# Linear attention, a channel MLP and a switched expert MLP on one core: GpSimd's drains tied to its loads, a clock for transfers, more slack for ScalarE in the order of side work

## The chip, the cores and the metric

The kernel runs on one core of one Trainium2 chip. The metric is the device time in microseconds (us), taken as the median of several runs. The core's engines each have an instruction queue of their own and work in order: TensorE (PE, matmuls), VectorE (DVE), ScalarE (ACT), GpSimd (POOL) and SyncE (SP, which here only issues transfers). They wait for each other through semaphores.

## The reference

Three stages follow each other. B=4 sequences, S=576 tokens, 8 heads of 64, model width 512.

```python
def phi(x):
    proj = einsum('bhsd,df->bhsf', x, w_phi)
    proj = proj - max(abs(proj), axis=-1)
    return concat([exp(proj), exp(-proj)])
num = q_p @ (k_p^T v);  den = q_p . sum(k_p) + 1e-6      # x = num / den
u = x + (x^T @ U @ V)^T
x = u + relu(u @ w_ch1) @ w_ch2                           # 512 -> 2048 -> 512
...
e = argmax(logits) or the token before's expert           # by a local gate
out = p[e] * (relu(x @ w1[e]) @ w2[e])                    # 512 -> 1024 -> 512, 8 experts
```

## The kernel before

**Stages.** Attention runs first, with the first pass of the channel MLP (FFN) already mixed into it. From about 207 us on, TensorE runs matmuls of passes one after another, 20 passes in all, numbered 0 to 19 here. Passes 0 to 11 are the FFN: 4 units of hidden channels (512 each) times 3 pieces of tokens (768 each). Passes 12 to 19 are the experts: for each of the 4 sequences, 2 units of 512 hidden channels of one expert. A pass is some 180 or 192 matmuls: the first product, ReLU, then the second product, `mm2`, whose results DVE adds into `y`. Passes 0 to 3 and all expert passes are plain (`plain_steps`, 192 matmuls); passes 4 to 11 use a seven-product scheme (`seven_steps`, 180 matmuls), in which DVE adds partial sums `u` in PSUM between the products.

**Number format.** Every operand of these matmuls is split into two float32r tiles, a high and a low part, so each product is three matmuls. The splits are the side work: ACT casts the high part (`CAST w<-row`, L338; `CAST x<-y`, L506), POOL or DVE subtracts it from the value to get the low part (`w<-row,w`, `x<-y,x`; POOL in halves, each a 128x256 instruction for weights). FFN weights arrive as 64-bit numbers and are first narrowed to float32 by six DVE operations (`narrow`, L88 to L101) and a POOL addition in two halves (`row<-row,row`). Split activations `x` are written to DRAM (`xd`) by SP and loaded again by POOL (`x_load`, L568, 768 KB each).

**The order.** Nothing is scheduled at run time. While the program is built, `work` emits TensorE's matmuls in order, and `side` after each step lets generators (`threads`) emit side work. They decide by a clock that the build keeps: `free[engine]` says when an engine would be done, `touched[tile]` when a tile would be ready. `gate` lets an instruction out if its engine would finish it by TensorE's clock plus `SLACK[engine][step]`, a table with one row per engine and a column per step (column 8 for all steps of a plain pass); `either` picks POOL or DVE by the earlier end, with a bias of 1.0 us against DVE. A transfer's landing is a guess at issue: TensorE's clock, or the tile's last use, plus 4.5, 5.0, 6.0 or 6.5 us.

**Drains.** `paused` issues POOL's elementwise instruction and, where `pauses[0]` is set (passes 0 to 2 and from pass 10 on), a POOL `drain` after it (L72).

**Buffers.** 8 `row` tiles for narrowing and sums, 14 weight tiles `w`, 9 activation tiles `x`, 8 PSUM banks `psf` used in rotation, and seven half buffers (`raw` and `row`) into which SP loads expert weights.

Of the kernel before, what the change touches and what calls it, by code (L numbers as in the profile page):

```python
# [39 lines left out]
def model(ctx, tc, kq, vx, wphi, ident, up, vp, wff, wg, wmoe1, wmoe2, rconst, outT):  # L40
    nc = tc.nc
# [12 lines left out]
    def f32(ap):  # L54
        return ap.bitcast(F32)
# [8 lines left out]
    rawfree = [raw_p.tile([128, 1024], U32, name=f"raw{n}") for n in range(2)]  # L64

    pauses = [False]

    def paused(eng, **kw):

        eng.tensor_tensor(**kw)  # L70
        if eng is nc.gpsimd and pauses[0]:
            nc.gpsimd.drain()  # L72

    def in_halves(eng, dst, a, b, n, op):
# [67 lines left out]
    def x_tile(pool, n):  # L142
# [7 lines left out]
    late = {}  # L150
# [8 lines left out]
    emitted = [0]  # L159
    SYNC = 0.15  # L160
    SLACK = {"DVE": (2.0, 0.4, 1.5, 0.3, 0.0, 0.0, 0.0, 1.0, 2.5, 2.5, 2.5, 2.5, 2.5, 2.5, 2.0),
             "ACT": (0.3, 1.0, 1.0, 1.0, 0.5, 0.0, 0.5, 1.0, 1.0, 1.0, 1.0, 1.0, 1.0, 1.0, 1.0),
             "POOL": (2.0,) * 15}
    BIAS = 1.0
    at_step = [7]
# [15 lines left out]
    def gate(eng, dur, *keys):  # L181

        if not late:
            yield "step"
        while late and not force[0]:
            at = max([free[eng]] + [touched.get(id(k), 0.0) for k in keys])
            if at + (0.0 if eng == "POOL" else dur) <= free["PE"] + SLACK[eng][at_step[0]]:
                break
            yield "wait"
        emitted[0] += 1  # L190
        force[0] = False
        if late:
            book(eng, dur, *keys)

    def either(eng, n, *keys):

        if not late:
            yield "step"
            emitted[0] += 1
            return eng  # L200
        while True:
            best = None
            for e, name, bias in ((nc.gpsimd, "POOL", 0.0), (nc.vector, "DVE", BIAS)):
                dur = cost(name, n)
                at = max([free[name], port[0]] + [touched.get(id(k), 0.0) for k in keys])
                ok = at + (0.0 if name == "POOL" else dur) <= free["PE"] + SLACK[name][at_step[0]]
                if (ok or force[0]) and (best is None or at + dur + bias < best[0]):
                    best = (at + dur + bias, e, name, dur)
            if best is not None:
                break  # L210
            yield "wait"
        emitted[0] += 1
        force[0] = False
        free[best[2]] = max(free[best[2]], port[0])
        port[0] = book(best[2], best[3], *keys)
        return best[1]

    def spawn(kind, due, gen):
        threads.append((due, len(threads) + 1000 * emitted[0], kind, gen))
# [43 lines left out]
    def later(on, issue):  # L263

        if late:
            waiting.append((touched.get(id(on), 0.0), issue))
        else:
            issue()
# [21 lines left out]
    def raw_dma():  # L290

        while order and rawfree and (not late or force[0] or touched.get(id(rawfree[0]), 0.0) <= free["PE"] + 0.5):
            u, name = order.pop(0)
            i = (BLOCKS + VS).index(name)
            t = rawfree.pop(0)
            if wff.dtype == F32:
                nc.sync.dma_start(out=t.bitcast(F32)[:, :512], in_=wff[u.g, i])
            else:
                nc.sync.dma_start(out=t, in_=wff[u.g, i].bitcast(U32))
            touched[id(t)] = max(free["PE"], touched.get(id(t), 0.0)) + 4.5  # L300
            raws.append((u, name, t))

    pieces = {}
# [138 lines left out]
    def w_moe(u, due):  # L442

        if not loading:
            assert not order and len(rawfree) == 2
            halfraw.extend(t.bitcast(F32)[:, 512 * m:512 * m + 512] for t in rawfree for m in range(2))
        if u.b not in ereg:
            ereg[u.b] = nc.sync.value_load(pidx[u.b][0:1, 0:1], min_val=0, max_val=NE - 1)
        e = bass.ds(ereg[u.b], 1)
        todo_ = list(PLAIN)  # L450
        ahead_ = []
        loading.append(todo_)
        while len(halfraw) < 7 and len(loading) == 1 and len(rows) > 5:
            halfraw.append(rows.pop()[:, :512])
        before = loading[:-1]

        def load():
            halfraw.sort(key=lambda t: touched.get(id(t), 0.0))
            while halfraw and todo_ and not any(before) and (force[0] or touched.get(id(halfraw[0]), 0.0) <= free["PE"] + 0.5):
                name = todo_.pop(0)  # L460
                t = halfraw.pop(0)
                if name[0] == "A":
                    j0, kh = 4 * u.g + 2 * (int(name[1]) - 1), int(name[2]) - 1
                    nc.sync.dma_start(out=t.rearrange("p (j c) -> p j c", j=2),
                                      in_=wmoe1[e, j0:j0 + 2, kh].rearrange("o j p c -> p (o j) c"))
                else:
                    nc.sync.dma_start(out=t, in_=wmoe2[e, 4 * u.g + int(name[1])].rearrange("o p f -> (o p) f"))
                touched[id(t)] = max(free["PE"], touched.get(id(t), 0.0)) + 5.0
                ahead_.append(t)

        def get(name):
            load()
            while not ahead_:
                yield "blocked"
                load()
            return ahead_.pop(0)

        for s in PLAIN:
            f = yield from get(s)
            spawn("w", due, w_end(u, s, f, nc.gpsimd, halfraw))  # L480
# [19 lines left out]
    def x_end(key, s, r, keep, own=None, then=None):  # L500

        x = xo.setdefault(key, {})[s] = yield from take(xfree)
        n_ = CH if key[0] == "m" else TW
        keys = (x,) if own is None else (x, own)
        yield from gate("ACT", cost("ACT", 2 * n_), *keys)
        nc.scalar.copy(out=x[:, 0, :, :n_], in_=r)  # L506
        for k in range(2):
            use = yield from either(nc.gpsimd, n_, *keys)
            paused(use, out=x[:, 1, k, :n_], in0=r[:, k], in1=f32(x[:, 0, k, :n_]), op=ALU.subtract)
        if keep:  # L510
            later(x, lambda: nc.sync.dma_start(out=f32(xd[key[1]][XD.index(s)]), in_=f32(x)))
        xdone.add((key, s))
        if then is not None:
            then()
# [10 lines left out]
    def x_sums(key, due):  # L525

        got = {}

        def load(s):
            r = got[s] = yield from take(rows)  # L530
            while touched.get(id(r), 0.0) > free["PE"] + 0.5 and not force[0]:
                yield "wait"
            k, t = spot(key, s)
            nc.sync.dma_start(out=as_x(r), in_=ud[:, k, t])
            emitted[0] += 1
            touched[id(r)] = max(free["PE"], touched.get(id(r), 0.0)) + 6.0

        def sub(out, a, c):
            for k in range(2):
                use = yield from either(nc.gpsimd, TW, out, a, c)  # L540
                paused(use, out=as_x(out)[:, k], in0=as_x(a)[:, k], in1=as_x(c)[:, k], op=ALU.subtract)

        def end(s, r, then=None):
            spawn("x", due, x_end(key, s, as_x(r), True, r, (lambda: rows.append(r)) if then is None else then))

        for s in ("B12", "B11", "B22"):
            yield from load(s)
        yield from sub(got["B11"], got["B12"], got["B11"])
        yield from sub(got["B12"], got["B22"], got["B12"])
        yield from sub(got["B22"], got["B22"], got["B11"])  # L550
        end("T2", got["B22"], lambda: None)
        end("T1", got["B11"])
        end("T3", got["B12"])
        yield from load("B21")
        yield from sub(got["B21"], got["B22"], got["B21"])
        while (key, "T2") not in xdone:
            yield "wait"
        rows.append(got["B22"])
        end("T4", got["B21"])

    def x_load(key, names=XS):

        for s in names:
            x = xo.setdefault(key, {})[s] = yield from take(xfree)
            while touched.get(id(x), 0.0) > free["PE"] + 0.3 and not force[0]:
                yield "wait"
            yield from gate("POOL", 1.0, x)
            nc.gpsimd.dma_start(out=x, in_=xd[key[1]][XD.index(s)])  # L568
            touched[id(x)] = max(free["PE"], touched.get(id(x), 0.0)) + 6.5
            xdone.add((key, s))  # L570

    def need_x(key, s):
# [763 lines left out]
    nc.vector.memset(late["lg"], 0.0)  # L1336
    nc.gpsimd.memset(late["tr"], 0.0)
    free.update(PE=0.0, DVE=0.0, ACT=1.0, POOL=2.0)
    touched.clear()
    for k in range(8):  # L1340
        ps_at[k] = 0.0
    for k in hat:
        hat[k] = 0.0
    nc.sync.dma_start(out=ud[:, :, 3 * S:], in_=y[:, :, 3 * S:])
    spawn("x", 2, x_plain(("p", 2), BS))
    spawn("w", 3, fetch(units[1], PLAIN))
    spawn("w", 3, w_ffn(units[1], 3))
    for _ in todo:
# [141 lines left out]
```

## Time and profile before

| | us |
|---|---|
| median of 3 runs (range) | 790.01 (789.01 to 790.75) |
| profiled execution, its own time | 789.29 |
| its span, first to last instruction | 787.5 |
| TensorE busy in it | 766.6 (97%) |
| DVE, ACT, POOL busy | 493.4, 300.4, 323.8 |
| mean granted TensorE clock | 0.995 |

TensorE is the engine to watch: with 97% busy, only what lies in its idle time, or in time at a lower clock, can be won without taking work away from it. A busy share of another engine says little by itself; what counts is the stretch in which TensorE waits for it.

### The profile page before, as it was taken

What the parts mean: (1) busy time and instruction counts of PE and PEld (TensorE: products, weight loads), DVE (VectorE), ACT (ScalarE), POOL (GpSimd) and SP (SyncE); (2) the same over time, 40 slices, a digit from 0 to 9 for tenths busy, and PEclk for the clock granted to TensorE, in tenths of its full rate; (3) what the DMA queues carried; (4) which work ended last, traced back from release to release, by engine and by line L of the source; (5) the groups of instructions that cost most, each with busy time, mean ns of one, the idle gap of its engine ahead of it and who ended that gap; (6) DMA issues with size and microseconds to landing.
All of it is one profiled execution on the core that took longest, in us unless ns stands there. A gap on an engine that the chain in (4) does not pass through costs nothing.

```text
span 787.5 us, 19160 instructions
## 1 busy us (share of the span) xinstructions
PE 766.6 (97%) x7776; PEld 742.8 (94%) x7776; DVE 493.4 (63%) x951; ACT 300.4 (38%) x682; POOL 323.8 (41%) x411
## 2 busy tenths in 40 slices
PE   8999999999999999799999999999999999999997
PEld 6899888999999998799999999999999999999997
DVE  7899999743388389768797865256653831615312
ACT  5667776652232131213123122023444353353330
POOL 0212423112257476764268442002436555555242
PEclk9999999999999999899999999999999999999999
DMA  6444556222243545683436527452443233523301
GB/s 198 151 124 164 204 177 224 67 101 82 101 159 99 211 174 196 253 283 138 171 110 219 224 81 234 164 164 81 130 172 108 87 109 96 179 82 90 123 19 63
DMA packets 45114, 114.33 MB, mean 145 GB/s; under 512 B 5024, under 2 KB 21536, under 8 KB 45024
## 3 DMA queue, kind: packets, MB, share of 16 engines
q1 hardware_dynamic: 36416, 82.74, 31.1%
q0 software_dynamic: 5152, 26.89, 10.2%
q10 hardware_dynamic: 3456, 3.46, 1.3%
q8 instruction: 62, 1.02, 0.5%
q14 instruction: 28, 0.23, 0.1%
HBM read 81.47 MB, written 31.60 MB: 144 GB/s over the span
## 4 chain that ended last, share of the span: by engine, by line
PE 69%; DVE 12%; issue 8%; POOLq 6%; ACT 2%; POOL 2%; DMA 1%; SPq 0%; DVEq 0%; ACTq 0%
PE psf L1077 9%; PE psf L1078 9%; PE psf L1079 9%; PE psf L961 9%; PE psf L962 8%; PE psf L963 8%; POOLq L72 6%; PE kv L699 4%; PE num L733 3%; PE pj L666 3%; PE tq L713 2%; DVE row L96 1%; DVE y L933 1%; DVE row L91 1%; PE tps L759 1%
## 5 line engine op out<-in xcount | busy, mean ns | idle before, releaser
L1077 PE MATMUL psf<-hhi,w 128*128 128x384 f32 (+1 forms) x640 | 204.8, 320 | 1.1 <-ACT w L338 0.6
L1078 PE MATMUL psf<-hhi,w 128*128 128x384 f32 (+1 forms) x640 | 203.8, 318 | 0.5 <-POOL w L70 0.5
L1079 PE MATMUL psf<-hlo,w 128*128 128x384 f32 (+1 forms) x640 | 203.7, 318 | 0.0
L961 PE MATMUL psf<-x,w 128*128 128x384 f32 (+1 forms) x608 | 195.5, 322 | 7.4 <-DVE u L933 5.0
L962 PE MATMUL psf<-x,w 128*128 128x384 f32 (+1 forms) x608 | 194.0, 319 | 0.0
L963 PE MATMUL psf<-x,w 128*128 128x384 f32 (+1 forms) x608 | 194.0, 319 | 0.0
L935 DVE SCALAR_TENSOR_TENSOR hlo<-psf,hhi 128x384 fp32r<-128x384 f32 (+1 forms) x160 | 78.8, 512 | 134.5 <-ACT hhi L949 134.5
L70 POOL TENSOR_TENSOR row<-row,row 128x256 f32<-128x256 f32 (+1 forms) x108 | 92.5, 876 | 115.0 <-DVE row L101 99.3
L949 ACT ACTIVATE hhi<-psf 128x384 fp32r<-128x384 f32 (+1 forms) x160 | 69.9, 462 | 181.8 <-PE psf L963 101.2
L961 PEld LDWEIGHTS psf<-x,w 128*128 128x128 f32 x608 | 114.7, 189 | 10.5 <-DVE u L933 5.7
L1077 PEld LDWEIGHTS psf<-hhi,w 128*128 128x128 f32 x640 | 120.1, 188 | 3.2 <-DVE hlo L935 1.3
L1078 PEld LDWEIGHTS psf<-hhi,w 128*128 128x128 f32 x640 | 120.1, 188 | 0.7 <-POOL w L70 0.7
L1079 PEld LDWEIGHTS psf<-hlo,w 128*128 128x128 f32 x640 | 120.1, 188 | 0.0
L962 PEld LDWEIGHTS psf<-x,w 128*128 128x128 f32 x608 | 114.8, 189 | 0.3 <-POOL x L70 0.3
L963 PEld LDWEIGHTS psf<-x,w 128*128 128x128 f32 x608 | 114.6, 189 | 0.0
L70 POOL TENSOR_TENSOR w<-row,w 128x256 fp32r<-128x256 f32 x96 | 75.0, 792 | 89.9 <-ACT w L338 42.7
L933 DVE TENSOR_TENSOR y<-psf,y 128x384 f32<-128x384 f32 (+1 forms) x128 | 66.6, 526 | 69.0 <-PE psf L1079 66.2
L70 POOL TENSOR_TENSOR x<-y,x 128x288 fp32r<-128x288 f32 (+1 forms) x50 | 47.2, 948 | 106.7 <-ACT x L506 100.2
L338 ACT CAST w<-row 128x512 fp32r<-128x512 f32 x61 | 35.6, 626 | 96.8 <-POOL row L70 41.2
L70 POOL TENSOR_TENSOR w<-raw,w 128x256 fp32r<-128x256 f32 x52 | 39.7, 764 | 42.8 <-ACT w L338 30.2
L669 DVE TENSOR_REDUCE mx<-pj 128x6 f32<-128x768 f32 (+2 forms) x49 | 45.8, 935 | 6.1 <-PE pj L666 6.1
L670 DVE TENSOR_TENSOR pg<-pj,mx 128x768 f32<-128x768 f32 (+2 forms) x49 | 46.1, 941 | 2.5
(111 smaller groups left out, 964.5 us busy)
## 6 DMA issues: line engine op xcount, KB each, us to landing
x<-xd POOLq DMA_DIRECT2D x34, 768.0 KB, 6.5
xd<-x SPq DMA_DIRECT2D x22, 768.0 KB, 4.2
raw<-in_wff SPq DMA_DIRECT2D x32, 512.0 KB, 3.6
raw<-in_wmoe SPq DMA_DIRECT2D x37, 256.0 KB, 3.2
kq<-in_kq SPq DMA_DIRECT2D x14, 576.0 KB, 3.9
row<-in_wmoe SPq DMA_DIRECT2D x27, 256.0 KB, 3.0
vt<-in_vx SPq DMA_DIRECT2D x16, 325.0 KB, 3.7
ud<-y SPq DMA_DIRECT2D x4, 1152.0 KB, 6.7
```

Of the source, the lines that this page charges most:

```text
L70: eng.tensor_tensor(**kw)
L72: nc.gpsimd.drain()
L670: nc.vector.tensor_tensor(out=p[:, :, sl], in0=ps[:, :, sl], in1=mx[:, :, sl].unsqueeze(3).to_broadcast([128, 2, m, 128]), op=ALU.subtract)
L933: nc.vector.tensor_tensor(**kw)
L935: nc.vector.scalar_tensor_tensor(op1=op1, **kw)
L949: at = act(lambda: nc.scalar.activation(out=hhi, in_=src, func=ACTF.Relu), n_, ready)
L961: nc.tensor.matmul(ps, lhsT=w[:, 0, c], rhs=x[:, 0, k, :n_], start=(first and k == 0), stop=False, skip_group_check=True)
L962: nc.tensor.matmul(ps, lhsT=w[:, 0, c], rhs=x[:, 1, k, :n_], start=False, stop=False, skip_group_check=True)
L963: nc.tensor.matmul(ps, lhsT=w[:, 1, c], rhs=x[:, 0, k, :n_], start=False, stop=(stop and k == 1), skip_group_check=True)
L1077: nc.tensor.matmul(ps, lhsT=wh, rhs=hhi, start=(k == 0), stop=False)
L1078: nc.tensor.matmul(ps, lhsT=wl, rhs=hhi, start=False, stop=False)
L1079: nc.tensor.matmul(ps, lhsT=wh, rhs=hlo, start=False, stop=(k == 3))
```

## The change

- `paused` drains POOL only if POOL's clock has reached `landed[0]`, the guessed landing of the last `x` load that POOL issued.
- A new function `transfer(kb, at)` keeps a clock `wire[0]` of all transfers at 400 KB per us and returns its end plus 2.5 us. The guessed landings become the later of that and the tile's last use plus 3.2 to 4.5 us. Writes of `x` to DRAM book `wire` too.
- ACT's row of `SLACK` rises from 1.0 to 1.8 in columns 1 to 3 and to 2.0 from column 7 on. The POOL gate ahead of an `x` load asks for 0.6 us instead of 1.0.
- The activations of token piece 2 are due at 3 instead of 2.

TensorE's instructions stand in the same order as before. On the other engines side work is moved.

```diff
+    landed, wire = [0.0], [0.0]
     def paused(eng, **kw):
         eng.tensor_tensor(**kw)
-        if eng is nc.gpsimd and pauses[0]:
+        if eng is nc.gpsimd and pauses[0] and free["POOL"] >= landed[0]:
             nc.gpsimd.drain()
...
-             "ACT": (0.3, 1.0, 1.0, 1.0, 0.5, 0.0, 0.5, 1.0, 1.0, 1.0, 1.0, 1.0, 1.0, 1.0, 1.0),
+             "ACT": (0.3, 1.8, 1.8, 1.8, 0.5, 0.0, 0.5, 2.0, 2.0, 2.0, 2.0, 2.0, 2.0, 2.0, 2.0),
...
+    def transfer(kb, at=None):
+        wire[0] = max(free["PE"] if at is None else at, wire[0]) + kb / 400
+        return wire[0] + 2.5
...
-            touched[id(t)] = max(free["PE"], touched.get(id(t), 0.0)) + 4.5
+            touched[id(t)] = max(transfer(512), touched.get(id(t), 0.0) + 3.8)
...
-                touched[id(t)] = max(free["PE"], touched.get(id(t), 0.0)) + 5.0
+                touched[id(t)] = max(transfer(256), touched.get(id(t), 0.0) + 3.2)
...
-            yield from gate("POOL", 1.0, x)
+            yield from gate("POOL", 0.6, x)
             nc.gpsimd.dma_start(out=x, in_=xd[key[1]][XD.index(s)])
-            touched[id(x)] = max(free["PE"], touched.get(id(x), 0.0)) + 6.5
+            landed[0] = touched[id(x)] = max(transfer(768, free["POOL"]), touched.get(id(x), 0.0) + 4.5)
...
+    landed[0] = wire[0] = 0.0
...
-    spawn("x", 2, x_plain(("p", 2), BS))
+    spawn("x", 3, x_plain(("p", 2), BS))
```

Three places show what moves. The first is POOL in pass 2, around its four loads of `x` for pass 3; drains are not among these rows, and in the kernel before one stands behind each half (x2 is two halves). Before:

```order
L70 TENSOR_TENSOR row3_87<-row3_87,row7_91 128x256 x2
L70 TENSOR_TENSOR row6_90<-row6_90,row4_88 128x256 x2
L568 DMA x8_3669<-xd0_106 128x1536
L568 DMA x3_105<-xd0_106 128x1536
L568 DMA x2_104<-xd0_106 128x1536
L568 DMA x1_103<-xd0_106 128x1536
L70 TENSOR_TENSOR row2_86<-row2_86,row7_91 128x256 x2
L70 TENSOR_TENSOR w13_3661<-row5_89,w13_3661 128x256 x2
L70 TENSOR_TENSOR row1_85<-row1_85,row7_91 128x256 x2
```

After the change, the same place:

```order
L578 DMA x8_3669<-xd0_106 128x1536
L578 DMA x3_105<-xd0_106 128x1536
L578 DMA x2_104<-xd0_106 128x1536
L578 DMA x1_103<-xd0_106 128x1536
L71 TENSOR_TENSOR w0_94<-row3_87,w0_94 128x256 x2
L71 TENSOR_TENSOR w12_3660<-row1_85,w12_3660 128x256 x2
L71 TENSOR_TENSOR row2_86<-row2_86,row5_89 128x256 x2
L71 TENSOR_TENSOR w1_95<-row0_84,w1_95 128x256 x2
L71 TENSOR_TENSOR row7_91<-row7_91,row3_87 128x256 x2
L71 TENSOR_TENSOR w4_98<-row2_86,w4_98 128x256 x2
```

Ten halves (those of `w0` to `row7`) follow the loads, and the program has no drain among them; the drains begin again with the halves of `w4`.

The second place is DVE from the end of pass 3 to the first `u` sums of pass 4 (`y<-psf` are pass 3's results, the rows from raw to row are narrowing). Before:

```order
L101 SCALAR_TENSOR_TENSOR row3_87<-raw1_93,row3_87 128x512
L88 TENSOR_SCALAR row5_89<-raw0_92 128x512
L933 TENSOR_TENSOR y_83<-psf_4648,y_83 128x384
L91 TENSOR_SCALAR row1_85<-row5_89 128x512
L94 TENSOR_SCALAR row5_89<-row1_85 128x512
L933 TENSOR_TENSOR y_83<-psf_4670,y_83 128x384
L96 SCALAR_TENSOR_TENSOR row5_89<-raw0_92,row5_89 128x512
L98 TENSOR_SCALAR row1_85<-row5_89 128x512
L101 SCALAR_TENSOR_TENSOR row1_85<-raw0_92,row1_85 128x512
L933 TENSOR_TENSOR u20_3675<-psf_4712,p10_3673 128x384
```

After:

```order
L102 SCALAR_TENSOR_TENSOR row5_89<-raw1_93,row5_89 128x512
L943 TENSOR_TENSOR y_83<-psf_4648,y_83 128x384
L338 TENSOR_TENSOR w6_100<-row1_85,w6_100 128x512
L338 TENSOR_TENSOR w7_101<-row4_88,w7_101 128x512
L943 TENSOR_TENSOR y_83<-psf_4669,y_83 128x384
L338 TENSOR_TENSOR row4_88<-row3_87,row4_88 128x512
L943 TENSOR_TENSOR u20_3675<-psf_4709,p10_3673 128x384
L943 TENSOR_TENSOR u21_3676<-psf_4716,p11_3674 128x384
L89 TENSOR_SCALAR row7_91<-raw0_92 128x512
```

The narrowing of the next weight block now stands behind the first two `u` sums, and three weight operations stand ahead of them.

The third place is ACT in the expert passes, where `w6` for pass 14 is cast (`hhi<-psf` are the ReLUs). Before, in pass 14 itself, behind its eight ReLUs:

```order
L949 ACTIVATE hhi_8027<-psf_8014 128x288
L949 ACTIVATE hhi_8044<-psf_8031 128x288
L949 ACTIVATE hhi_8069<-psf_8056 128x288
L338 CAST w6_100<-raw1_93 128x512
L338 CAST w10_3658<-raw1_93 128x512
L338 CAST w1_95<-row5_89 128x512
```

After, in pass 13, between its ReLUs:

```order
L959 ACTIVATE hhi_7662<-psf_7649 128x288
L344 CAST w7_101<-row0_84 128x512
L344 CAST w0_94<-row1_85 128x512
L959 ACTIVATE hhi_7687<-psf_7674 128x288
L1158 ACTIVATE r_ex_7705<-r_sh_7704 128x40
L344 CAST w5_99<-raw0_92 128x512
L344 CAST w8_3656<-raw0_92 128x512
L344 CAST w6_100<-raw1_93 128x512
L959 ACTIVATE hhi_7729<-psf_7716 128x288
```

Casts of expert weights now stand between ReLUs, about a pass earlier; with them, many subtractions of weights in passes 12 to 17 move from DVE to POOL.

## Rows read from the trace of the kernel before

**Rows 1.** The page: span, share of TensorE, the granted clock in 40 slices

```profile
span 787.5 us, 19160 instructions
PE 766.6 (97%) x7776; PEld 742.8 (94%) x7776; DVE 493.4 (63%) x951; ACT 300.4 (38%) x682; POOL 323.8 (41%) x411
PEclk9999999999999999899999999999999999999999
```

**Rows 2.** Busy time by pass: 3, 4, 5, 7, 9, 14, 15; length, PE, PEld, DVE, ACT, POOL, clock

```profile
273.43:307.26 33.83, 33.69 (x194) 33.37 (x193) 29.38 (x47) 7.75 (x14) 22.62 (x28) 1.00 0.42 147
307.26:348.21 40.95, 33.77 (x181) 32.50 (x181) 30.73 (x55) 9.08 (x17) 30.59 (x38) 0.92 0.76 270
348.21:380.21 32.00, 31.49 (x181) 31.17 (x181) 23.10 (x41) 8.35 (x18) 13.31 (x17) 1.00 0.42 142
...
411.67:443.25 31.58, 31.50 (x181) 31.18 (x181) 25.70 (x48) 7.35 (x14) 20.86 (x24) 1.00 0.71 261
...
474.62:505.84 31.22, 31.22 (x182) 31.22 (x181) 13.50 (x26) 4.89 (x11) 5.18 (x9) 1.00 0.61 208
...
628.58:655.47 26.89, 25.82 (x195) 25.37 (x193) 8.70 (x23) 13.71 (x32) 15.43 (x21) 1.00 0.44 123
655.47:680.75 25.28, 25.28 (x195) 25.28 (x193) 13.12 (x22) 9.20 (x19) 16.02 (x18) 1.00 0.43 132
```

**Rows 3.** TensorE's waits: line, releaser, us in total, times, longest

```profile
PE psf L961 <- DVE u L933: 5.0, 1, 5.0
PE psf L961 <- DVE y L933: 2.2, 3, 1.6
PE psf L1077 <- ACT w L338: 0.6, 1, 0.6
PE psf L1077 <- DVE hlo L935: 0.5, 1, 0.5
PE psf L1078 <- POOL w L70: 0.5, 1, 0.5
```

**Rows 4.** TensorE in time, around 321.65: start, length, what [idle before]

```profile
316.29 0.34 PE L963 MATMUL psf<-x,w 128*128 128x384 f32 x1
321.65 0.69 PE L961 MATMUL psf<-x,w 128*128 128x384 f32 x1 [5.02 <-DVE u L933]
322.13 0.52 PE L962 MATMUL psf<-x,w 128*128 128x384 f32 x1
322.45 0.52 PE L963 MATMUL psf<-x,w 128*128 128x384 f32 x1
```

**Rows 5.** POOL in time in pass 2, its elementwise halves and four loads

```profile
257.15 0.89 POOL L70 TENSOR_TENSOR row<-row,row 128x256 f32<-128x256 f32 x1 [0.16 <-POOL row L70]
258.20 0.74 POOL L70 TENSOR_TENSOR row<-row,row 128x256 f32<-128x256 f32 x1 [0.16 <-POOL row L70]
259.55 2.49 POOL L568 DMA_DIRECT2D x<-xd  x4 [0.61 <-issue]
262.01 0.79 POOL L70 TENSOR_TENSOR row<-row,row 128x256 f32<-128x256 f32 x1
271.71 0.74 POOL L70 TENSOR_TENSOR row<-row,row 128x256 f32<-128x256 f32 x1 [8.91 <-issue]
```

**Rows 6.** The drains of L72, 258 to 275 us: ns least, median, most

```profile
L72 POOLq DRAIN  x6: 827/908/10080, 257.1 to 273.6; - x6
```

**Rows 7.** DVE in time, from pass 2 into pass 3

```profile
261.42 0.42 DVE L88 TENSOR_SCALAR row<-raw 128x512 uint32<-128x512 uint32 x1
272.48 0.43 DVE L91 TENSOR_SCALAR row<-row 128x512 f32<-128x512 f32 x1 [10.65 <-POOL row L70]
...
278.15 2.40 DVE L933 TENSOR_TENSOR y<-psf,y 128x384 f32<-128x384 f32 x5
280.48 0.54 DVE L935 SCALAR_TENSOR_TENSOR hlo<-psf,hhi 128x384 fp32r<-128x384 f32 x1
```

**Rows 8.** DVE by line and form, 290 to 322: count, busy us, mean ns, idle before

```profile
L70 DVE TENSOR_TENSOR x<-row,x 128x384 fp32r<-128x384 f32 x5 | 4.5, 922 | 0.0
L933 DVE TENSOR_TENSOR y<-psf,y 128x384 f32<-128x384 f32 x8 | 4.4, 548 | 0.0
L91 DVE TENSOR_SCALAR row<-row 128x512 f32<-128x512 f32 x4 | 3.6, 902 | 1.3 <-POOL row L70 1.3
L88 DVE TENSOR_SCALAR row<-raw 128x512 uint32<-128x512 uint32 x3 | 3.6, 1195 | 0.0
L70 DVE TENSOR_TENSOR row<-row,row 128x384 f32<-128x384 f32 x2 | 3.2, 1650 | 2.8 <-POOL row L70 2.8
L96 DVE SCALAR_TENSOR_TENSOR row<-raw,row 128x512 uint32<-128x512 uint32 x4 | 2.8, 698 | 0.0
L94 DVE TENSOR_SCALAR row<-row 128x512 uint32<-128x512 uint32 x4 | 2.8, 694 | 0.1
```

**Rows 9.** DVE and POOL in time about 308 to 313

```profile
307.64 2.74 DVE L88 TENSOR_SCALAR row<-raw 128x512 uint32<-128x512 uint32 x1
308.35 1.04 POOL L70 TENSOR_TENSOR x<-row,x 128x384 fp32r<-128x384 f32 x1
309.33 3.65 POOL L70 TENSOR_TENSOR row<-row,row 128x256 f32<-128x256 f32 x4
```

**Rows 10.** POOL by line and form in expert passes, 573 to 756 us

```profile
L70 POOL TENSOR_TENSOR w<-raw,w 128x256 fp32r<-128x256 f32 x42 | 32.3, 770 | 33.0 <-ACT w L338 21.8 <-issue 4.7 <-POOL w L70 4.2
L70 POOL TENSOR_TENSOR y<-y,row 128x288 f32<-128x288 f32 x24 | 22.8, 951 | 9.7 <-DVE y L933 6.8 <-issue 2.9
```

**Rows 11.** ACT in time in pass 14

```profile
641.41 0.41 ACT L949 ACTIVATE hhi<-psf 128x288 fp32r<-128x288 f32 x1 [1.17 <-PE psf L963]
641.72 1.13 ACT L338 CAST w<-raw 128x512 fp32r<-128x512 f32 x2
```

**Rows 12.** The page's transfers: count, size, median us to landing

```profile
x<-xd POOLq DMA_DIRECT2D x34, 768.0 KB, 6.5
raw<-in_wmoe SPq DMA_DIRECT2D x37, 256.0 KB, 3.2
```

More of the change, by code (lines that the diff above doesn't have):

```diff
@@ L510, in x_end, with send @@
         if keep:
-            later(x, lambda: nc.sync.dma_start(out=f32(xd[key[1]][XD.index(s)]), in_=f32(x)))
+            def send():
+                nc.sync.dma_start(out=f32(xd[key[1]][XD.index(s)]), in_=f32(x))
+                if late:
+                    transfer(768)
+            later(x, send)
         xdone.add((key, s))
@@ L535, in load @@
             emitted[0] += 1
-            touched[id(r)] = max(free["PE"], touched.get(id(r), 0.0)) + 6.0
+            touched[id(r)] = max(transfer(384), touched.get(id(r), 0.0) + 3.5)
         def sub(out, a, c):
```

## Prediction

> **What bounds the kernel now.** I read the page first: TensorE is busy 766.6 of 787.5 us, and the granted clock is full in all 40 slices but one [rows 1]. So the change, which leaves TensorE's instructions and their order alone, can win only idle or slow time of TensorE. The table of busy time by pass says where that is [rows 2]. A seven-product pass that nothing disturbs takes 31.22 us (pass 9), a plain expert pass 25.28 us (pass 15). Over 180 and 192 matmuls that is 0.1735 and 0.1317 us each, so a plain FFN pass of 192 wide matmuls needs 192 x 0.1735 = 33.3 us. Against these, pass 3 has 0.5 us too much, pass 4 9.7 (40.95 - 31.22), pass 5 0.8, pass 7 0.4 and pass 14 1.6 (26.89 - 25.28). With about 0.4 for passes 6 and 8 that makes 13.4 us; everything else runs at its matmul count, and attention, ahead of pass 1, keeps its order. No result below 789.3 - 13.4 = 775.9 can come from this change.
>
> Nearly three quarters of it is pass 4. Its clock column reads 0.92 where the neighbours have 1.00 [rows 2]. The list of waits puts one of 5.0 us on a partial sum `u` of DVE and 2.2 us in three on DVE's `y` [rows 3]; all four lie between 310.9 and 321.7 us. After the long one a matmul starts 0.32 us after the one ahead of it instead of 0.17 [rows 4]: for some nine matmuls TensorE ran near its lower level, 1.2 of 2.4 GHz, having stood idle for 5.02 us. That is 9 x (0.32 - 0.17) = 1.4 us. 5.0 + 2.2 + 1.4 and some 1.1 of short waits are the 9.7.
>
> Why DVE is late there is found two passes earlier. In pass 2, POOL issues four loads of `x` at 259.55 us; the half behind them starts at 262.01 and the next at 271.71, after 8.91 us idle, while halves elsewhere follow at 0.16 us [rows 5]. Between the two stands a drain; six drains there have a median of 908 ns, half included, and one has 10080 [rows 6]. Two of these loads' medians of 6.5 us [rows 12] would cover 259.55 to 271.62. So the trace shows this drain ending when the loads have landed. DVE, which needed that half, stood idle for 10.65 us [rows 7] and came out about 7 us behind: it does the last `y` sums of pass 2 at 278 to 280 us, while pass 3 began at 273.43. It then runs nearly full (29.38 us busy of 33.83, 30.73 of 40.95 [rows 2]) and can't make that up.
>
> **The change part by part.** *The drain.* Behind the four loads there are now ten halves without a drain, and the loads stand earlier. A half is 0.74 to 0.79 us [rows 5], so the ten occupy POOL for some 8 us, and the cast that the next drained tile, `w4`, waits for comes at the end of the pass. By then the loads of 12.1 us should have landed. So the 8.91 us on POOL and the 10.65 us on DVE go, and DVE enters pass 3 up to 7 us less late. More drains stand elsewhere in the changed program (235 against 197). The 0.16 us between halves stays, so they are costed at nothing as long as POOL has slack, which it has outside pass 2 to 4 and the expert passes.
>
> What is late next is DVE itself. I counted its instructions from a point 13.0 us into pass 3, where it can't start earlier, to the second `u` sum of pass 4, due 18 matmuls into that pass: 36.4 - 13.0 = 23.4 us. In the changed order these are 12 sums of `y`, `hlo` and `u` at 0.55, 6 subtractions at 0.92, 3 weight operations (priced as the same) and 17 narrowing operations at a mean of 0.76, all from the stretch in which DVE and POOL fought for SBUF [rows 8]: 6.6 + 5.5 + 2.8 + 12.9 = 27.8. Neighbours overlap by 0.07 (280.55 against 280.48 in [rows 7]), 38 times: 25.1. That is 1.7 us too much. At quiet durations (0.48 for a sum, 0.43 for an operation of 512 columns [rows 7], the six kept at 0.92) it is 5.8 + 5.5 + 1.3 + 7.3 - 2.7 = 17.2, 6 us to spare. TensorE's own margin at that point is about 2 us: 18 matmuls or 3.1 us, less two sums, 1.1. So the lower bound of what stays is nothing. For the upper bound I add the waits of DVE for POOL, 2.8 + 1.3 [rows 8], should they come back: 1.7 + 4.1 - 2.0 = 3.8, plus 1.4 of slow clock if it is one wait, 5.2. I take 1.0, near the lower end, because DVE loses most where POOL's halves run without a gap [rows 9], and these now lie in pass 2. To that I add 0.3 at the second product of pass 4, where five narrowing operations stand ahead of three sums; pass 7, which has the like, lost 0.4 in all. Pass 4 so gives 9.7 - 1.3 = 8.4, and pass 3 its 0.5.
>
> *ScalarE further ahead.* In pass 14 the cast of `w6` starts at 641.72, right behind the last ReLU at 641.41 [rows 11], and TensorE waits for `w` of ACT (0.6), for POOL's low part (0.5) and for `hlo` (0.5) [rows 3], together the 1.6. In the new order this cast stands between ReLUs of pass 13, some 150 matmuls or 19 us ahead of its use. The 1.6 go. The price is that a cast, 1.13 us for two and so about 0.57, delays a ReLU; group 4 of a unit's ReLUs ends at matmul 72 and is needed at 100, 28 x 0.1317 = 3.7 us later, less ReLU 0.41 [rows 11] and `hlo` 0.54 [rows 7], so 2.7 of margin hide up to four casts. If a cast waits for its transfer, that cover is gone: the second rival below.
>
> *POOL takes over from DVE in passes 12 to 18.* Weight halves on POOL go from 118 to 160 there, 42 x (0.77 + 0.16) = 39 us [rows 5, 10]. POOL is busy about 16 of 25.3 us of a pass [rows 2] and, with some 23 halves at 0.93 a pass and the `y` sums of pieces at 0.95, would be near 97% in the fullest. Lower parts that come late would cost their lateness, up to the 3.2 us of a transfer; with 19 us of lead I take nothing.
>
> *The transfer clock* itself issues nothing. It moves the guessed landings, and with them casts and subtractions; I see passes 5 and 7 gain (0.8 and 0.4 lost before, 0.7 and 0.3 taken as won, since the stretches get freer of contention), 6 and 8 nothing.
>
> **Sum.** 0.5 + 8.4 + 0.7 + 0.3 + 1.6 = 11.5 us, so the profiled execution falls from 789.3 to 777.8. That execution stands 0.7 under the median of 790.0, hence a median of 778.5. If all goes right it is 776.6.
>
> **The rivals.** *One: DVE stays late, because undrained POOL halves hold it up.* Beside four back-to-back halves of 3.65 us an L88 on DVE took 2.74 us [rows 9], where it takes 0.42 alone [rows 7]: 2.3 lost. Ten such halves would cost DVE 5.8 us in pass 2, fully blocked 10 x 0.81 = 8.1, against 10.65 before. Pass 4 then gives back only 10.65 - 5.8 = 4.9 or 10.65 - 8.1 = 2.5, and with the 2.6 of passes 5, 7 and 14 the time is 782.5 to 785. For it: DVE has no slack in passes 3 and 4. Against it: DVE's work in pass 2 isn't all of the form that suffers, `y` sums read PSUM, and DVE before did nothing at all in those 10 us.
> The Trainium skill, "SBUF — State Buffer", section "SBUF: two separate sides", speaks for this rival: the port pair that DVE and GpSimd share is an exclusive lock for a whole instruction, and the loser blocks fully. By that rule the 2.3 us of that L88 are a wait and not a slower read, and the sum comes out at the 785 end; the trace agrees in that L88's 2.74 us, but subtractions in the same stretch took 0.92 on the mean, so it does not show a block each time.
>
> *Two: slower, through ScalarE's queue in the expert passes.* A cast that stands between ReLUs and waits for a weight transfer holds all ReLUs behind it. Transfers take 3.2 us at the median [rows 12]; two in a row hold ACT 6.4, which is 3.7 beyond the 2.7 of margin. If that comes once in each of passes 12 to 18, the time is 778.5 + 7 x 3.7 = 804; from some 1.6 us a pass on, the whole gain is gone. For it: ACT ran with little ahead of it and casts are now let out on a guess (256 KB at 400 KB per us plus 2.5, so 3.1 us, where the median is 3.2). Against it: the half buffers allow the loads to start up to a pass earlier, and ACT is busy only 9 to 14 us of a pass [rows 2].
>
> *Three: the change doesn't do what it says.* The guess for a load of 768 KB is 768/400 + 2.5 = 4.4 us for the first one, against 6.5 [rows 12]. If a drain still meets loads under way, the stall moves and stays; only passes 5, 7 and 14 gain, 2.6 us: 787.4. For it: the four loads took 12.1 us together and the clock gives the last of them 10.2. Against it: the ten halves and the cast ahead of `w4`.
>
> **How the numbers follow.** Forecast 0.60, one 0.20, two 0.07, three 0.08, anything else 0.05. Less than 0.2% (1.6 us) can't be told from no change here. The forecast and one are faster; three straddles that line, half each; of the rest 0.02 is faster and 0.03 the same. That gives 0.86, 0.07 and 0.07. The range runs from the best case less the spread of runs (776.6 - 1.1) to beyond the far end of rival one, 785 + 1: 775.5 to 786.0. Left out are rivals two and three and the tails.
>
> **What will show it.** Right: no drain over 2 us in passes 2 and 3, DVE's gap of 10.65 us gone, `y` sums of pass 2 ending within 4 us of pass 3's start, pass 4 at 32 to 33 us with clock 1.00 and no wait over 2 us, pass 14 at 25.3. Rival one: halves on POOL without gaps beside DVE operations of 1.5 to 3 us in pass 2, and pass 4 at 36 us or more. Two: passes 12 to 18 above 26 us, with TensorE waiting for ACT's ReLUs and ACT for SP's transfers. Three: a drain of 5 us or more. My number is wrong above all if the contended 25.1 us on DVE is the true one and POOL's waits come back, or if the drains that are new elsewhere fall on loads.

## The result and the profile after

The changed kernel takes 782.08 us (median of 6 runs, 780.91 to 783.45) where the kernel before took 790.09 beside it: a ratio of 0.990, with a 95% interval of 0.989 to 0.991. That is 8.0 us gained, where 11.5 were forecast; the time lies inside the range of 775.5 to 786.0. The profiled execution took 781.76 us, with a span of 779.7.

The page shows the shorter span, and a clock that is full in all 40 slices (against [rows 1]).

```profile
span 779.7 us, 19252 instructions
PE 763.8 (98%) x7776; PEld 741.6 (95%) x7776; DVE 482.7 (62%) x921; ACT 300.7 (39%) x682; POOL 362.2 (46%) x463
PEclk9999999999999999999999999999999999999999
```

Busy time by pass, for passes 3, 4, 5, 7 and 14 (length, PE, PEld, DVE, ACT, POOL, granted clock, DMA share, GB/s), answers to [rows 2]:

```profile
272.65:305.95 33.30, 33.30 (x194) 33.30 (x193) 26.59 (x39) 8.96 (x16) 21.29 (x24) 1.00 0.42 139
305.95:339.50 33.55, 31.55 (x181) 31.12 (x181) 29.57 (x47) 8.09 (x15) 23.60 (x26) 1.00 0.69 247
339.50:373.29 33.79, 31.77 (x182) 31.13 (x181) 26.56 (x45) 8.53 (x18) 16.83 (x22) 1.00 0.46 175
404.76:436.93 32.17, 31.50 (x182) 31.19 (x181) 24.08 (x43) 7.42 (x14) 24.10 (x30) 1.00 0.66 214
622.11:647.39 25.28, 25.28 (x195) 25.28 (x193) 7.74 (x19) 14.18 (x33) 18.92 (x24) 1.00 0.38 113
```

Pass 4 fell from 40.95 to 33.55 us, pass 3 from 33.83 to 33.30, pass 14 from 26.89 to 25.28. Pass 5 grew from 32.00 to 33.79 and pass 7 from 31.58 to 32.17. These sum to 7.2; another 0.7 lies ahead of pass 1, in attention (pass 0 is mixed into it), where no instruction moved. Over the traces of this document that stretch takes 206.0 to 209.2 us, so the 0.7 can be chance.

POOL around its four loads in pass 2 (start, length, what, idle before), and the drains of 239 to 277 us (count, shortest, median and longest in ns), answers to [rows 5, 6]:

```profile
253.58 2.36 POOL L578 DMA_DIRECT2D x<-xd  x4 [0.60 <-issue]
255.92 3.62 POOL L71 TENSOR_TENSOR w<-row,w 128x256 fp32r<-128x256 f32 x4
259.51 1.78 POOL L71 TENSOR_TENSOR row<-row,row 128x256 f32<-128x256 f32 x2
```

```profile
L73 POOLq DRAIN  x17: 814/839/1241, 239.9 to 276.2; - x17
```

The idle of 8.91 us is gone and no drain takes over 1.3 us. What TensorE still waits for (us in total, times, longest), an answer to [rows 3]:

```profile
PE psf L971 <- DVE u L943: 3.0, 3, 2.0
PE psf L1087 <- DVE hlo L945: 1.6, 1, 1.6
```

The 2.0 lies at 314.35 us in pass 4, behind a DVE that had run without a break from 295.4 us on. The 1.6 lies at 356.5 in pass 5; ahead of it DVE ran without a break from 331.4 to 353.6 us and then waited twice for a ReLU. In that second stretch two DVE operations stand out, one at the end of pass 4 and one in pass 5. DVE in time, then POOL beside it:

```profile
334.50 4.49 DVE L89 TENSOR_SCALAR row<-raw 128x512 uint32<-128x512 uint32 x1
...
348.43 2.63 DVE L338 TENSOR_TENSOR w<-row,w 128x512 fp32r<-128x512 f32 x1
```

```profile
333.64 1.10 POOL L578 DMA_DIRECT2D x<-xd  x2
334.75 3.94 POOL L71 TENSOR_TENSOR x<-row,x 128x384 fp32r<-128x384 f32 x4
...
344.26 1.10 POOL L578 DMA_DIRECT2D x<-xd  x2
345.37 3.74 POOL L71 TENSOR_TENSOR w<-row,w 128x256 fp32r<-128x256 f32 x4
349.07 1.43 POOL L71 TENSOR_TENSOR row<-row,row 128x256 f32<-128x256 f32 x2
```

An L89 takes 0.42 us where POOL is quiet. This one began while POOL issued its second load and ended at 338.99, just after the four halves behind the loads (338.69). The next question was whether such runs make up what is missing, and whether the drain was the loss in pass 4 at all.

### The profile page after: what moved, and what is told of

It reads as the page before. It is cut to its first block, busy times and chain, and to the rows that moved or that the text cites. A ratio compares the mean times of both kernels' runs of the same rounds, so it can differ in the third digit from the quotient of the medians.

```text
span 779.7 us, 19252 instructions
## 1 busy us (share of the span) xinstructions
PE 763.8 (98%) x7776; PEld 741.6 (95%) x7776; DVE 482.7 (62%) x921; ACT 300.7 (39%) x682; POOL 362.2 (46%) x463
## 3 DMA queue, kind: packets, MB, share of 16 engines
q0 software_dynamic: 5152, 26.89, 10.2%
## 4 chain that ended last, share of the span: by engine, by line
PE 82%; DVE 9%; issue 4%; POOL 2%; ACT 2%; POOLq 0%; DMA 0%; DVEq 0%; ACTq 0%
PE psf L1087 11%; PE psf L1089 11%; PE psf L1088 11%; PE psf L972 11%; PE psf L971 11%; PE psf L973 10%; PE kv L709 4%; PE pj L676 3%; PE num L743 3%; PE tq L723 2%; POOL row L71 1%; PE tps L769 1%; PE utps L786 1%; DVE row L89 1%; DVE pg L680 1%
## 5 line engine op out<-in xcount | busy, mean ns | idle before, releaser
L71 POOL TENSOR_TENSOR w<-row,w 128x256 fp32r<-128x256 f32 x122 | 97.3, 809 | 92.8 <-ACT w L344 39.1
L71 POOL TENSOR_TENSOR row<-row,row 128x256 f32<-128x256 f32 (+1 forms) x105 | 89.1, 869 | 99.4 <-DVE row L102 91.1
L71 POOL TENSOR_TENSOR x<-y,x 128x288 fp32r<-128x288 f32 (+1 forms) x56 | 51.9, 930 | 85.2 <-ACT x L512 78.2
L71 POOL TENSOR_TENSOR w<-raw,w 128x256 fp32r<-128x256 f32 x72 | 54.5, 757 | 32.6 <-ACT w L344 16.1
```

## The experiments

Lengths of the passes that differ, in us (an undisturbed one: pass 3 33.30, passes 4, 5 and 7 31.22, pass 14 25.28), and the median against the kernel before on the same chip. The lengths come from one profiled execution of each kernel, the medians from all of its runs:

| kernel | pass 4 | pass 5 | pass 7 | pass 14 | median | ratio to before (95%) |
|---|---|---|---|---|---|---|
| before | 40.95 | 32.00 | 31.58 | 26.89 | 790.09 | |
| changed | 33.55 | 33.79 | 32.17 | 25.28 | 782.08 | 0.990 (0.989 to 0.991) |
| condition alone | 37.47 | 31.98 | 31.57 | 26.89 | 786.11 | 0.994 (0.992 to 0.995) |
| order alone | 35.06 | 32.99 | 31.22 | 25.28 | 783.15 | 0.991 (0.989 to 0.993) |
| changed, drains in all passes | 34.29 | 33.69 | 31.22 | 25.28 | 782.95 | 0.990 (0.989 to 0.992) |
| changed, no drains | 33.55 | 33.93 | 32.15 | 25.28 | 784.57 | 0.992 (0.991 to 0.994) |
| changed, loads on SP, drains in all | 33.37 | 31.22 | 31.22 | 25.28 | 780.24 | 0.987 (0.985 to 0.989) |
| changed, loads on SP | 32.97 | 31.22 | 31.22 | 25.28 | 778.46 | 0.986 (0.983 to 0.989) |
| before + ACT's row | 41.53 | 31.22 | 31.57 | 25.28 | 797.04 | 1.009 (1.007 to 1.011) |
| changed, ACT's old row | 32.62 | 33.65 | 32.11 | 25.28 | 782.07 | 0.989 (0.987 to 0.991) |
| before, loads on SP | 35.57 | 31.97 | 31.22 | 26.88 | 783.95 | 0.991 (0.989 to 0.992) |
| changed, ACT's old row, loads on SP | 32.61 | 32.59 | 31.22 | 25.28 | 779.61 | 0.986 (0.984 to 0.987) |
| guesses alone | 39.17 | 31.73 | 32.11 | 25.28 | 785.93 | 0.993 (0.991 to 0.995) |
| guesses and gate | 38.23 | 33.61 | 32.13 | 25.28 | 787.65 | 0.996 (0.994 to 0.997) |

**The two halves of the change.** First the drain condition without the new order, then the order without the condition.

```diff
-        if eng is nc.gpsimd and pauses[0]:
+        if eng is nc.gpsimd and pauses[0] and free["POOL"] >= landed[0]:
```

> The kernel before with the new drain condition alone (its transfer clock only decides which drains fall away; no other instruction moves): seven halves instead of none follow the four loads of pass 2 without a drain. Theory A (the drain that waits for loads is the loss of pass 4): pass 4 falls from 40.95 to 33 to 35 us, DVE's gap of 10.65 us goes, pass 14 keeps its 1.6 us of excess, time 782 to 784.5. Rival B (it is the new order, with loads earlier and less DVE work ahead of the sums): the stall only moves by some halves, time 787 or more.

> The changed kernel with a drain behind every POOL half again in the passes that had them, so that only the order of side work differs from the kernel before. Theory A: the drain behind the loads of 253.6 us waits some 9 us again, DVE stands idle about as long as before, pass 4 is 38 us or more, pass 14 is repaired all the same (25.3), time 786 to 789. Rival B: with the loads 6 us earlier the stall finds DVE with time to spare, time 782 to 784.

Neither theory holds as it stood, though the rival's time for the order alone (782 to 784) came out. The condition alone takes 3.5 us from pass 4, the order alone 5.9, both together 7.4: they are largely substitutes. With the order alone the stall is as long as before, but the loads stand some 5 us earlier and it ends earlier, 267.67 against 272.48 in [rows 7], and DVE has caught up by pass 4 but for 2.0 us. The longest drain there (ns), and DVE behind it:

```profile
L73 POOLq DRAIN  x28: 812/842/10466, 240.0 to 279.2; - x28
```

```profile
267.67 0.43 DVE L92 TENSOR_SCALAR row<-row 128x512 f32<-128x512 f32 x1 [8.21 <-POOL w L71]
```

These 2.0 us are the same wait as in the changed kernel. Pass 4 is 1.5 us longer because TensorE ran slower behind it: from 1.1 us after the wait on, matmuls started 0.32 us apart instead of 0.17, ten times, near the lower clock level of 1.2 GHz. In the changed kernel the clock stayed full. Pass 4 with the order alone (length, PE, PEld, DVE, ACT, POOL, granted clock, DMA share, GB/s):

```profile
307.20:342.26 35.06, 33.06 (x181) 32.74 (x181) 29.73 (x48) 8.15 (x15) 23.16 (x26) 0.95 0.71 261
```

The 95% intervals of the two ratios overlap as well, so it is not shown that the condition is worth anything on top of this order.

With the condition alone DVE entered pass 3 on time, and TensorE waited 4.4 us for `u` all the same. DVE lost its lead inside pass 3, behind a load and four halves without drains (POOL, then DVE, then TensorE's wait):

```profile
280.23 0.57 POOL L577 DMA_DIRECT2D x<-xd  x1 [0.54 <-issue]
280.82 3.94 POOL L71 TENSOR_TENSOR row<-row,row 128x384 f32<-128x384 f32 x4
```

```profile
280.36 4.70 DVE L95 TENSOR_SCALAR row<-row 128x512 uint32<-128x512 uint32 x1
```

```profile
PE psf L971 <- DVE u L943: 4.4, 1, 4.4
```

**Drains elsewhere.** To see whether runs of halves without a gap hold DVE, drains were put into passes 3 to 9, and in another kernel taken out everywhere (`False` in the same line).

```diff
-        pauses[0] = i < NP or i > nf - NP
+        pauses[0] = True
```

> The changed kernel with drains (under the new condition) in passes 3 to 9 too, order unchanged. Theory C (what is still lost in passes 4, 5 and 7, 5.9 us, is DVE held up by halves that follow each other on POOL without a gap: an L89 of 4.49 us beside four halves at 334.5 us, a weight subtraction of 2.63 us beside four more at 348.4): the L89 takes under 1.5 us, pass 5 falls from 33.8 to about 31.7, time 778.5 to 780. Rival D (the new order puts too much work of DVE ahead of the sums): the waits stay, time 781.5 to 782.5. A third way: the added drains meet loads of x under way and stall POOL again, 783 or more.

> The changed kernel with no drain between POOL's halves in any pass, order unchanged. Theory C: narrowing operations of DVE of 1.5 to 4 us beside runs of halves also in passes 0 to 3, DVE enters pass 4 later, time 1 to 5 us above the changed kernel's 782.1. Rival D: drains matter only where they wait for loads, time within 0.7 us of 782.1.

The first did not decide; its 782.95 lies between the ranges of the rival and of the third way. Under the condition the runs behind loads stay without drains, and the same four halves again held one DVE operation, here for 4.35 us; pass 7 came clean, pass 5 did not, and two drains that met a load under way took 4.6 and 4.3 us (POOL, then DVE):

```profile
336.32 1.10 POOL L578 DMA_DIRECT2D x<-xd  x2 [0.53 <-issue]
337.43 3.93 POOL L71 TENSOR_TENSOR x<-row,x 128x384 fp32r<-128x384 f32 x4
```

```profile
337.56 4.35 DVE L97 SCALAR_TENSOR_TENSOR row<-raw,row 128x512 uint32<-128x512 uint32 x1
```

Without any drains the passes are as long as with them to 0.2 us. The median, 2.5 us above the changed kernel's, lies where theory C put it and not within the 0.7 of D; but in the trace the 2.9 us of longer span lie ahead of pass 1 (1.2), where both kernels have no such drains, and after the last matmul (1.6). So the drains as such are worth nothing to TensorE in these passes, and theory C's forecast of a DVE that enters pass 4 later was wrong, for the wait there is 2.0 us again. What makes this kernel's runs longer is not shown.

**The loads on another queue.** If a load on POOL's queue is what makes a drain wait and a run hold DVE, the same order with the loads issued by SP must lose both.

```diff
-            nc.gpsimd.dma_start(out=x, in_=xd[key[1]][XD.index(s)])
+            nc.sync.dma_start(out=f32(x), in_=f32(xd[key[1]][XD.index(s)]))
```

> The changed kernel with the loads of x issued by SP instead of POOL, so that no drain can meet a load of POOL's own, and a drain behind every POOL half in all passes; order of side work unchanged. The pair with the next run tests theory C where the run with drains in all passes could not: there the two runs of four halves stood behind loads again and stayed without drains (DVE took 4.35 and 2.62 us beside them). Theory C (back-to-back halves hold DVE): no DVE operation above 2 us in passes 3 to 5, pass 5 about 31.5 us, pass 4 32 to 33, time 777.5 to 779.5. Rival D (too much DVE work ahead of the sums): pass 5 stays above 33, time 781 to 783. A third way: loads queue behind waiting transfers on SP and TensorE waits for x: 784 or more.

> The same with SP's loads, but drains only in the passes that have them in the kernel before (0 to 2 and from 10), without the new condition. Both theories: no drain above 1.3 us in pass 2, DVE's idle of 8 us in the run of the order alone is gone, pass 4 33 to 35. Theory C: runs of halves without a gap in passes 3 to 9 still hold DVE for 2.5 to 4.5 us, pass 5 stays near 33.8, time 781 to 783. Rival D: the same time as the run before this one within 0.7 us.

Passes 5 and 7 come clean in both, with and without drains there; pass 4 keeps 1.8 to 2.2 us. The second is 1.8 us faster, but its trace shows 2.2 us less ahead of pass 1 and 0.4 less in pass 4. Theory C in its first form, any back-to-back halves, falls with the second kernel, for it has the same runs without drains. There DVE goes between the same four halves instead of waiting for all (POOL, then DVE):

```profile
335.00 4.49 POOL L71 TENSOR_TENSOR x<-row,x 128x384 fp32r<-128x384 f32 x4
```

```profile
335.06 1.24 DVE L89 TENSOR_SCALAR row<-raw 128x512 uint32<-128x512 uint32 x1 [0.73 <-POOL row L71]
336.33 1.12 DVE L92 TENSOR_SCALAR row<-row 128x512 f32<-128x512 f32 x1
337.49 1.12 DVE L95 TENSOR_SCALAR row<-row 128x512 uint32<-128x512 uint32 x1
```

Then the same edit in the kernel before, whose order is otherwise kept:

> The kernel before with one edit: SP issues the loads of x instead of POOL; order of side work, guesses and drains as before. Theory G (formed after the two runs with SP's loads, in which no DVE operation took over 1.7 us: a load on POOL's own queue costs twice, as a drain that waits for it and as a run of halves behind it that holds DVE to its end; the order of side work only decides how much of this reaches TensorE): no drain over 1.4 us, DVE's 10.65 us gap gone, pass 4 at 33 to 35.5, pass 14 still 26.9, time 780 to 783. Theory E (DVE's load in pass 3 in the old order is the cause by itself): pass 4 stays at 36 or more, time 784 or more.

One line takes 5.4 us from pass 4 and gives a ratio of 0.991, about that of the whole change. Its 35.57 lies just above what theory G allowed and just under what the rival did, and so does its time. No DVE operation is held any more and no drain waits, and still the old order keeps 4.4 us in pass 4: 2.5 of wait, the rest at a lower clock (0.95 on the mean). So both count. TensorE's wait:

```profile
PE psf L961 <- DVE u L933: 2.5, 1, 2.5
```

**Which edit makes the order.** ACT's row alone, then everything but that row.

> The kernel before with ACT's new SLACK row alone: no transfer clock, no drain condition. Theory E (after the runs of the condition alone and of the order alone: it is DVE's load in pass 3, and so the order, that decides, and ACT's slack makes the order): pass 14 at 25.3, pass 4 36 us or less, time 783 to 785. Rival F (the transfer clock makes the order that matters): pass 14 repaired, pass 4 39 us or more, 787 to 789.

> The changed kernel with ACT's SLACK row of before: transfer clock, drain condition, 0.6 us gate and later due time stay. Theory E: pass 14 loses its 1.6 us again and pass 4 stands at 36 us or more, time 785 to 787. Rival F: pass 14 at 26.9, pass 4 at 33 to 34, time 782.5 to 784.

Both theories missed the first: the row alone makes the kernel slower by 7 us. Pass 1 took 40.72 us instead of 33.30, since a low part of `x` came late from POOL, and pass 4 41.53. TensorE's waits in this kernel:

```profile
PE psf L961 <- DVE u L933: 8.6, 1, 8.6
PE psf L962 <- POOL x L70: 5.2, 1, 5.2
```

The second is as fast as the whole change, so ACT's row is not needed for it. Pass 14 reads 25.28 in both, which neither theory expected of the second: the new row and the new guesses each suffice to cast `w6` in time. The rest was taken apart once more, without that row and without the condition; in this order the later due time of piece 2 moves no DVE or POOL instruction in the built program. With ACT's new row it does move some, POOL's low parts of `x` among them, and the row was not run together with it. So the loss of 7 us is shown for the row with the earlier due time only.

> The kernel before with the transfer clock's guessed landings alone: no drain condition, SLACK row, gate of 1.0 us and due time of before. If the guesses make the part of the order that matters: pass 14 at 25.3 and pass 4 at 35 to 37, time 782.5 to 785. If the later due time of the activations is what lets DVE catch up: a stall of a drain over 8 us and pass 4 at 38 or more, time 786 to 789.

> The changed kernel without the drain condition and without ACT's new SLACK row: guessed landings and the gate of 0.6 us ahead of the loads of x (the later due time moves no instruction). Beside the run without the new row it differs by the condition alone, beside the run of the guesses alone by the gate alone. If the drain condition is worth most in this order: a drain of 8 us or more, DVE idle as long, pass 4 at 38 to 40 us, time 787 to 789. If loads that the gate lets go earlier, and so an earlier stall, suffice as in the run of the order alone: pass 4 at 34 to 36, time 783 to 785.

Without the condition a drain of 7.9 and one of 6.4 us come back, and pass 4 stands at 39.17 and 38.23. Against the same order with the condition (32.62) it is worth 5.6 us in pass 4, 3.6 of wait and 2.0 of slower matmuls, where on top of the order that ACT's row makes the wait was 2.0 us with it and without it. What the condition is worth thus depends on the order; that it hangs on how far behind the stall leaves DVE is argued, not shown. The longest drain of the last kernel and DVE's wait in it:

```profile
L73 POOLq DRAIN  x35: 812/836/6439, 239.4 to 286.1; - x35
```

```profile
269.70 0.43 DVE L89 TENSOR_SCALAR row<-raw 128x512 uint32<-128x512 uint32 x1 [6.27 <-POOL row L71]
```

**A faster version.** SP's loads without ACT's new row were run as well:

> The changed kernel with SP's loads, drains as in the kernel before, and ACT's SLACK row of before. Both theories: like the run with SP's loads and the new row (778.5) within 1 us; pass 4 at 32 to 33, pass 5 at 31.2, pass 14 at 25.3. If the new row has a use of its own, some pass is longer than there.

It takes 779.61 us, at a ratio of 0.986 (0.984 to 0.987), below the changed kernel's interval; with the new row the median is 778.46. Pass 5 keeps 1.4 us without the row and none with it, though the two ratios are the same. TensorE's longest wait after attention is then the `u` of pass 4, 1.1 and 1.5 us.

## Why the prediction was right, and where it was not

The direction, the place and the range held; the size was 3.5 us too large. By the terms of its sum:

- **Pass 3 (0.5) and pass 14 (1.6)** came as forecast. For pass 14 the cause named, ScalarE further ahead, is sufficient but not needed: with ACT's old row the new guesses do the same.
- **Pass 4 (8.4)** gave 7.4. DVE's stretch into it was put between 17.2 and 25.1 us. From 13.0 us into pass 3 to the second `u` sum DVE was busy 26.7 (the row below), more than the upper bound. The wait left is 2.0, where 1.0 was taken; the upper end of 5.2 was not reached. The mechanism was only half of it, and that the size came near is in part luck: the drain's stall was read as the loss of pass 4, but with the stall removed and the old order kept, 6.3 of its 9.7 us stayed, and the new order won 5.9 with the stall in place. Of the 6.3, about 1.9 go when SP issues the loads and no DVE operation is held; 4.4 are left in the old order even so.
- **Passes 5 and 7 (0.7 and 0.3)** is the step that failed. They lost 1.8 and 0.6 more instead, 3.4 of the 4.0 us that the profiled execution misses. The ground given was that contention falls. In the new order DVE operations meet runs of halves behind POOL's loads (4.49 us at 334.50; 2.51 at 408.46, ahead of a `u` wait of 0.67 in pass 7), and a weight subtraction of 2.63 us stands ahead of sums. Nothing in the sum had a price for a load as such. The row for it was there: the L88 of 2.74 us in [rows 9], at 307.64, began while POOL issued two loads (the second row below), which the text did not look for.
- **Rival one** had the mechanism of the missing part, in the wrong place. In pass 2, beside the ten halves, no narrowing operation took over 1.12 us and pass 4 was far from 36; the held operations came in passes 3 to 7, most of them right behind loads. The rule of the Trainium skill that was cited there ("SBUF — State Buffer", section "SBUF: two separate sides", a lock held for one instruction) does not tell the two apart: DVE was held for four instructions behind a load on POOL, and for about one at a time with the loads on SP.
- **Rival two** did not happen: passes 12 to 18 are as long as before to 0.1 us, but for the gain in pass 14. **Rival three** neither; the longest drain in pass 2 is 1.24 us.

The changed kernel from 13.0 us into pass 3 to the second `u` sum (length, PE, PEld, DVE, ACT, POOL, granted clock, DMA share, GB/s), and POOL's loads at 307.25 us in the kernel before:

```profile
285.65:314.76 29.11, 27.11 (x156) 26.79 (x156) 26.68 (x40) 6.85 (x12) 22.85 (x25) 1.00 0.71 257
```

```profile
307.25 1.10 POOL L568 DMA_DIRECT2D x<-xd  x2
```

Not settled is why a run behind a load holds DVE to its end. A load is not always needed: the 2.63 us at 348.43 began 3.1 us after one ended. Nor is it always enough: the ten halves of pass 2 in the changed kernel stand right behind four loads, and DVE went between them. Nor was it tried which other edit would take the last 1 to 2 us out of pass 4.

## What to carry to other kernels

Here a GpSimd drain behind loads that GpSimd had issued waited for them, and DVE, once late, made TensorE wait two passes later. Before such a stall is priced at the wait it ends in, ask what else holds the late engine, since two causes of one wait don't add. Where GpSimd shares its time between elementwise work and loads, try the loads on another queue first: one line was worth as much here as a re-planned order, and with that order more.

## What the runs showed of the hardware

In the kernels with POOL's loads, DVE operations that take 0.4 to 0.9 us otherwise took up to 5.0 in many places where they began during or right after a load issue on POOL with two to six halves behind it; most ended 0.2 to 0.6 us after the last of these halves. In all four kernels whose loads SP issues, no elementwise DVE operation after 200 us took over 1.7 us, though the halves, and in three of the four the runs without drains, were the same in kind; a load took 6.1 to 8.1 us at the median on SP's queue, against 6.1 to 6.7 on POOL's. Without drains in the expert passes a DVE operation on 8 elements took 7.68 us beside POOL, whose halves stood back to back; in the changed kernel it takes 0.22 to 0.26. DVE, then POOL, of the kernel with no drains:

```profile
637.69 7.68 DVE L1216 TENSOR_SCALAR r_po<-rc_sb,r_pf 1x8 f32<-1x8 f32 x1
```

```profile
636.66 5.62 POOL L71 TENSOR_TENSOR w<-raw,w 128x256 fp32r<-128x256 f32 x8
642.25 3.86 POOL L71 TENSOR_TENSOR x<-y,x 128x288 fp32r<-128x288 f32 x5
```

The drain of 10.08 us in the kernel before [rows 6] ran from 261.54 to 271.62 us. The last of the four loads ahead of it was issued at 261.5 and landed after 9.9 us, at 271.4. The loads (issue durations in ns, first and last start), and their time to landing:

```profile
L568 POOL DMA_DIRECT2D x<-xd x4: 557/568/872, 259.5 to 261.5; - x4
...
DMA to landing us min/median/max: 4.9/7.4/9.9
```

Behind a wait of 2.0 us at the same matmul of pass 4 the granted clock fell in the trace of the order alone (0.95 over the pass) and stayed full in that of the changed kernel (1.00).
